# Moving every buffer that feeds TensorE to a multiple of 128 bytes in SBUF, in a fused convolution, GLU and squared-ReLU kernel

## The chip, the cores and the metric

One NeuronCore of a Trainium2 chip runs the whole program. The metric is device time in microseconds (us); lower is better. Three timed runs of the kernel before gave 2457.78, 2458.15 and 2459.22 us, so the median is 2458.15 us. The execution that the profiler recorded took 2455.46 us in all, of which the trace spans 2453.6 us.

## The reference

The input is `x` of shape (4, 4096, 192), four sequences of 4096 tokens. Three layers follow one another, all in fp32:

```python
w = softmax(weight, axis=-1)                 # (8 heads, 7 taps); 24 channels share a head
x1[s] = sum_k w[head, k] * x[s - 6 + k]      # causal convolution over the sequence, zeros before it
y   = (sigmoid(x1 @ w_gate) * (x1 @ w_val)) @ w_out          # 192 -> 1536 -> 192
out = (relu(y @ w_in2) ** 2) @ w_out2                        # 192 -> 2048 -> 192
```

Nearly all arithmetic is in the five matrix products over 16384 tokens.

## The kernel before

**Precision.** TensorE is fed with a rounded 4-byte type (`F32R`). A factor is split into a high part (the rounded value) and a low part (what rounding left), and a product is the sum of three: high by high, low of the moving operand by high weight, high by low weight. The matmuls accumulate the three in PSUM.

**Tiles.** Tokens are taken in 32 tiles of `NT = 512`. The channels lie on the partitions and the 512 tokens along them, so that one moving operand is 512 elements of 4 bytes, 2048 bytes in each partition. Every matmul of the three layers uses 64 partitions. They come in pairs: one for partitions 0 to 63, the next for 64 to 127, each with its own weights and its own PSUM bank, and the two run side by side in the two halves of the array.

**Units and phases.** A phase is one tile in one layer. A tile of the first layer (kind 1) has 12 units of 128 hidden channels, a tile of the second (kind 2) has 8 units of 256. `rows(u)` (L417) multiplies the tile's moving operand `x` with the unit's weights: 18 matmuls, that is 9 pairs. `activate(u)` (L438) turns the PSUM banks into hidden values `s` on ScalarE and VectorE, and splits them into `gh` (L455, ScalarE) and `gl` (L456, VectorE). `cols(u)` (L461) multiplies `gh` and `gl` with the output weights: 5 pairs for a unit of kind 1, 10 pairs for one of kind 2. When a phase has ended, `fold` (L485) adds the accumulators up. The program first runs three phases of kind 1, then one phase of each kind in turn, and last three phases of kind 2. The order on every engine is the order in which the program is written (`manual_schedule`): `rows` of a unit goes ahead of `cols` of a unit one or two earlier, and small works (`side`) are hung on the units.

**The moving buffers.** `operands` (L82) has two slots for the split tile `x`, each `[P, 6, 512]`. They are handed out in turn (`Slots`, L66). From the fourth phase on, the tiles of kind 1 always get the one and those of kind 2 the other, until only phases of kind 2 are left and the slots alternate. `gh` and `gl` have five buffers each. The weights lie in `w1`, `wr2` and `wo2`.

**The convolution.** `convolve` (L304) transposes the tile into `xT`, which has 6 history columns ahead of 512 new ones. `turn` copies the history in, `keep` saves the last 6 columns into a small buffer `ha`, both on GpSimd. There is one `ha` for channels 0 to 127 of the even tiles, one for those of the odd tiles, and one for the other channels. The taps follow on VectorE (L328), or, for the very first tiles, as matmuls with diagonal weights (L337, plain fp32).

**Addresses.** A pool places its buffers one behind the other in the order in which they are first asked for, each rounded up to 32 bytes. In the program before, this gives the following starts in each partition (the last column is the start modulo 128):

```
w1             16512    0        cp: small ones end at 121376  (32)
wr2            71808    0        xT of A       133664   32     2072 bytes, takes 2080
wo2            96384    0        ha (three)    24 bytes, take 32 each
x, slot 0     139936   32        xT of B       137824   96     2072 bytes, takes 2080
x, slot 1     152256   64        s  (3)   172736 ...  64
gh (5)        178880   64        gl (5)   189120 ...  64
```

Slot 0 is the one that serves the phases of kind 2 in the long middle part; slot 1 serves those of kind 1.

Of the kernel before, what the change touches and what calls it, by code (L numbers as in the profile page):

```python
# [8 lines left out]
F32 = mybir.dt.float32  # L9
# [7 lines left out]
P = 128  # L17
HB = 64
NT = 512
BLK = 32  # L20
HALVES = (slice(0, HB), slice(HB, P))


@with_exitstack
def kernel(
# [25 lines left out]
    H, K = weight.shape  # L51
    GRP = D // H
    PAD = K - 1
    F1, F2 = w_gate.shape[1], w_in2.shape[1]
    NU1, NU2 = F1 // P, F2 // (2 * P)
    TOK = B * S
# [3 lines left out]
    cp = ctx.enter_context(tc.tile_pool(name="cp", bufs=1))  # L60
    xp = ctx.enter_context(tc.tile_pool(name="xp", bufs=1))
# [113 lines left out]
    def chunk_loads(raw, srcs):  # L175
# [5 lines left out]
            )  # L181
            for half, src in zip(HALVES, srcs)
        ]
# [75 lines left out]


    xin, halo, x1, x2 = {}, {}, {}, {}

    def tokens(t):
        p, i = divmod(t, 2)
        q, j = divmod(p, TPB)
        return (2 * q + i) * S + j * NT
# [30 lines left out]
    def diagonal(i, k):  # L297
        return diag[2 * i + k // 4][:, k % 4, :]
# [5 lines left out]
    def convolve(nm, seqs, raw, j, on_array):  # L304

        i = "AB".index(nm)
        st = {}

        def turn():
            xt = st["x"] = xp.tile([P, PAD + NT], F32, tag="xT" + nm, name="xT" + nm)  # L310
            if j == 0:
                nc.vector.memset(xt[:, 0:PAD], 0.0)
            else:
                nc.gpsimd.tensor_copy(xt[:, 0:PAD], halo[nm, seqs])
            nc.vector.transpose(xt[:, PAD : PAD + NT], raw())

        def keep():
            if j < TPB - 1:
                h = halo[nm, seqs] = xp.tile([P, PAD], F32, tag=f"ha{nm}{seqs}", name="ha" + nm)
                nc.gpsimd.tensor_copy(h, st["x"][:, NT : NT + PAD])  # L320

        def first():
            st["cv"] = xp.tile([P, NT], F32, tag="cv" + nm, name="cv" + nm)
            nc.scalar.activation(st["cv"], st["x"][:, 0:NT], AF.Copy, scale=cw[:, i, 0:1])
            keep()

        def tap(k):
            nc.vector.scalar_tensor_tensor(  # L328
                out=st["cv"], in0=st["x"][:, k : k + NT], scalar=cw[:, i, k : k + 1],
                in1=st["cv"], op0=ALU.mult, op1=ALU.add,  # L330
            )

        def products():
            st["bank"] = banks.take("cv")
            st["cv"] = st["bank"][1]
            for k in range(K):
                nc.tensor.matmul(  # L337
                    st["cv"], diagonal(i, k), st["x"][:, k : k + NT],
                    start=(k == 0), stop=(k == K - 1),
                )  # L340
            keep()

        if on_array:
            return st, [turn, products]
        return st, [turn, first] + [lambda k=k: tap(k) for k in range(1, K)]

    def done(st):
# [7 lines left out]
    def part_ops(t, into, nm, src_a, src_b, done):  # L355

        own, other = HALVES[t % 2], HALVES[1 - t % 2]

# [15 lines left out]
        def spread():  # L374
            xs = into[t][1].bitcast(F32)
            nc.sync.dma_start(out=xs[HALVES[0], 4:6, :], in_=xs[HALVES[1], 0:2, :])
            nc.sync.dma_start(out=xs[HALVES[1], 4:6, :], in_=xs[HALVES[0], 0:2, :])
            nc.sync.dma_start(out=xs[other, 2:4, :], in_=xs[own, 2:4, :])
# [38 lines left out]
    def rows(u):  # L417
# [7 lines left out]
        for i, (c, o, p) in enumerate(steps):  # L425
            for h, half in enumerate(HALVES):
                nc.tensor.matmul(  # L427
# [33 lines left out]
    def cols(u):  # L461
# [4 lines left out]
        if u.f == 0:  # L466
            acc[key] = [[banks.take(f"acc{nm}") for nm in "AB"] for _ in HALVES]
        sums = acc[key]
# [238 lines left out]
```

## Time and profile before

| | |
|---|---|
| median of three timed runs | 2458.15 us |
| the profiled execution | 2455.46 us, span 2453.6 us |
| PE busy | 2395.8 us, 98% of the span, 20512 matmuls |
| PEld busy (weight loads) | 1936.4 us, 79% |
| DVE, ACT, POOL busy | 69%, 53%, 1% |
| granted TensorE clock, mean | 0.992 of full speed |

Busy time of PE is modelled and neighbouring matmuls overlap: one matmul of 64 by 512 is shown with about 390 ns, though a new pair starts every 0.23 us. The pace of TensorE is therefore read from starts, or from the chain of waits, where each piece is as long as it kept the chain. PE names matmuls and PEld the weight loads before them; `x` is the split tile, `pg`, `pv` and `ph` are PSUM banks of `rows`, `accA` and `accB` those of `cols`.

### The profile page before, as it was taken

Reading aid. Unit: us, or ns where it says so; the run is one execution under the profiler, and the core shown is the slowest. Engines: PE = TensorE matmul, PEld = TensorE weight load, DVE = VectorE, ACT = ScalarE, POOL = GpSimd, SP = SyncE. Lnnn points to the kernel's source line nnn. Section 1 sums busy time; section 2 is a strip of 40 time slices with the busy share of each in tenths; the row PEclk is TensorE's granted clock in tenths of the full one; section 3 lists DMA queues with packets and bytes.
Section 4 is the critical chain, followed back from the end, with each engine's and each line's share of the span. In section 5 each row is a group of like instructions: output and inputs, shape, how many; then the busy total and the mean of one; then the engine's idle time right before and its main releaser. Section 6 shows DMA issues by size and latency. Waiting matters only on the chain.

```text
span 2453.6 us, 49309 instructions
## 1 busy us (share of the span) xinstructions
PE 2395.8 (98%) x20512; PEld 1936.4 (79%) x20512; DVE 1704.9 (69%) x2676; ACT 1308.5 (53%) x2260; POOL 24.8 (1%) x97
## 2 busy tenths in 40 slices
PE   6898999999999999999999999999999999999998
PEld 3576888888888888888888888888888888888886
DVE  5776767676776766767676776766767676776676
ACT  5555555554555554555554555554555554555564
POOL 1000000000000000000000000000000000000000
PEclk8999999999999999999999999999999999999999
DMA  6232111112111121211112111121211112111111
GB/s 126 65 78 57 40 23 31 33 34 42 38 21 35 29 38 38 40 23 31 33 34 42 38 20 36 29 38 38 41 22 31 34 33 42 38 21 27 25 35 27
DMA packets 226896, 92.12 MB, mean 38 GB/s; under 512 B 202857, under 2 KB 214257, under 8 KB 226673
## 3 DMA queue, kind: packets, MB, share of 16 engines
q1 hardware_dynamic: 226272, 88.39, 17.8%
q8 instruction: 160, 2.62, 0.4%
q0 software_dynamic: 256, 0.52, 0.1%
q14 instruction: 64, 0.52, 0.1%
q10 hardware_dynamic: 144, 0.07, 0.0%
HBM read 26.03 MB, written 12.58 MB: 16 GB/s over the span
## 4 chain that ended last, share of the span: by engine, by line
PE 91%; DVE 4%; ACT 2%; issue 1%; DMA 1%; SPq 0%; DVEq 0%; ACTq 0%
PE pg L427 29%; PE accA L479 24%; PE ph L427 22%; PE accB L479 16%; DVE s L445 1%; ACT gh L455 1%; PE pv L427 1%; DVE gl L456 1%; DVE cvA L328 0%; DMA raw<-in_moe_w_out_dram 0%; ACT s L444 0%; DMA x<-x 0%; PE cv L337 0%; DVE cvB L328 0%; DVE w L168 0%
## 5 line engine op out<-in xcount | busy, mean ns | idle before, releaser
L427 PE MATMUL pg<-x,w 64*128 64x512 f32 x3456 | 866.3, 393 | 26.5 <-ACT w L157 22.4
L427 PE MATMUL pv<-x,w 64*128 64x512 f32 x3456 | 863.1, 393 | 14.2 <-DMA x<-x 10.3
L455 ACT CAST gh<-s 128x512 fp32r<-128x512 f32 x896 | 555.6, 621 | 520.0 <-DVE s L445 401.6
L456 DVE TENSOR_TENSOR gl<-s,gh 128x512 fp32r<-128x512 f32 x896 | 608.0, 692 | 286.2 <-ACT gh L455 264.0
L427 PEld LDWEIGHTS pg<-x,w 64*128 64x128 f32 x3456 | 639.3, 186 | 168.4 <-ACT w L157 27.1
L427 PEld LDWEIGHTS pv<-x,w 64*128 64x128 f32 x3456 | 639.7, 186 | 31.6 <-DVE s L445 11.6
L427 PE MATMUL ph<-x,wr 64*128 64x512 f32 x4608 | 573.4, 391 | 0.0
L427 PEld LDWEIGHTS ph<-x,wr 64*128 64x128 f32 x4608 | 431.9, 184 | 103.1 <-DVE s L445 0.4
L448 DVE TENSOR_TENSOR s<-s 128x512 f32<-128x512 f32 x512 | 330.3, 686 | 150.6 <-ACT s L447 149.7
L479 PE MATMUL accA<-gh,wo 64*128 64x512 f32 x2048 | 402.8, 390 | 0.0
L447 ACT ACTIVATE s<-ph 128x512 f32<-128x512 f32 x512 | 277.5, 594 | 214.6 <-PE ph L427 213.9
L445 DVE TENSOR_TENSOR s<-pv,s 128x512 f32<-128x512 f32 x384 | 263.2, 685 | 184.5 <-ACT s L444 184.0
L444 ACT ACTIVATE s<-pg 128x512 f32<-128x512 f32 x384 | 228.1, 594 | 245.5 <-PE pv L427 238.0
L479 PE MATMUL accA<-gh,w 64*128 64x512 f32 x1536 | 312.0, 390 | 0.0
L479 PEld LDWEIGHTS accA<-gh,wo 64*128 64x128 f32 x2048 | 192.3, 184 | 44.4
L479 PE MATMUL accA<-gl,wo 64*128 64x512 f32 x1024 | 200.4, 388 | 0.0
L479 PE MATMUL accB<-gh,wo 64*128 64x512 f32 x1024 | 200.4, 388 | 0.0
L479 PE MATMUL accB<-gl,wo 64*128 64x512 f32 x1024 | 199.9, 387 | 0.0
L479 PEld LDWEIGHTS accA<-gh,w 64*128 64x128 f32 x1536 | 157.5, 185 | 31.6 <-ACT gh L455 0.2
L479 PE MATMUL accA<-gl,w 64*128 64x512 f32 x768 | 158.5, 389 | 0.2 <-DVE gl L456 0.2
L479 PE MATMUL accB<-gh,w 64*128 64x512 f32 x768 | 158.0, 388 | 0.0
L479 PE MATMUL accB<-gl,w 64*128 64x512 f32 x768 | 157.9, 388 | 0.0
(92 smaller groups left out, 1442.4 us busy)
## 6 DMA issues: line engine op xcount, KB each, us to landing
x<-x SPq DMA_DIRECT2D x192, 256.0 KB, 3.8
out_dram<-oA SPq DMA_DIRECT2D x128, 64.0 KB, 2.0
xiA<-in_x_dram SPq DMA_DIRECT2D x124, 64.0 KB, 3.6
out_dram<-oB SPq DMA_DIRECT2D x64, 64.0 KB, 2.0
xiB<-in_x_dram SPq DMA_DIRECT2D x60, 64.0 KB, 2.8
rawr<-in_moe_w_in_dram SPq DMA_DIRECT2D x16, 192.0 KB, 3.4
rawo<-in_moe_w_out_dram SPq DMA_DIRECT2D x16, 192.0 KB, 2.5
raw<-in_moe_w_gate_dram SPq DMA_DIRECT2D x12, 192.0 KB, 3.3
```

Of the source, the lines that this page charges most:

```text
L427: nc.tensor.matmul(u.banks[h][1], w[half, o + c * P : o + (c + 1) * P], xs[1][half, place[c][h] + p, :], start=(i == 0), stop=(i == len(st ...
L444: nc.scalar.activation(s, u.banks[0][1], AF.Sigmoid)
L445: nc.vector.tensor_tensor(s, u.banks[1][1], s, op=ALU.mult)
L447: nc.scalar.activation(s, u.banks[i][1], AF.Relu)
L448: nc.vector.tensor_tensor(s, s, s, op=ALU.mult)
L455: nc.scalar.copy(v.gh, s)
L456: nc.vector.tensor_tensor(v.gl, s, v.gh.bitcast(F32), op=ALU.subtract)
L479: nc.tensor.matmul(sums[h][b][1], wt[half], m[half], start=(first and k in (0, 3)), stop=(last and k in (2, 4)),)
```

## The change

The transposed tile `xT` is made 544 columns wide instead of 518 (2176 bytes), of which the columns behind 518 are never touched. The three history buffers become one buffer `halos` of `[P, 3, 6]`, and it is taken from the pool of constants `cp`. No instruction is added, removed or moved, and none works on other elements than before; only addresses differ.

```diff
+LINE = 32
...
+    XT = NT + LINE * -(-PAD // LINE)
...
     xin, halo, x1, x2 = {}, {}, {}, {}
+    halos = cp.tile([P, 3, PAD], F32, name="halos")
...
         def turn():
-            xt = st["x"] = xp.tile([P, PAD + NT], F32, tag="xT" + nm, name="xT" + nm)
+            xt = st["x"] = xp.tile([P, XT], F32, tag="xT" + nm, name="xT" + nm)
...
         def keep():
             if j < TPB - 1:
-                h = halo[nm, seqs] = xp.tile([P, PAD], F32, tag=f"ha{nm}{seqs}", name="ha" + nm)
+                h = halo[nm, seqs] = halos[:, 2 * "AB".index(nm) + seqs, :]
                 nc.gpsimd.tensor_copy(h, st["x"][:, NT : NT + PAD])
```

## Rows read from the trace of the kernel before

**Rows 1.** The page: busy time of each engine, share of the span.
```profile
span 2453.6 us, 49309 instructions
PE 2395.8 (98%) x20512; PEld 1936.4 (79%) x20512; DVE 1704.9 (69%) x2676; ACT 1308.5 (53%) x2260; POOL 24.8 (1%) x97
```

**Rows 2.** The page: the chain that ended last, by engine.
```profile
PE 91%; DVE 4%; ACT 2%; issue 1%; DMA 1%; SPq 0%; DVEq 0%; ACTq 0%
```

**Rows 3.** Busy time by stage: microseconds and number of instructions, granted clock, DMA share.
```profile
30.00:90.00 60.00, 38.66 (x247) 25.61 (x245) 35.40 (x70) 32.77 (x46) 0.69 (x4) 0.86 0.45 104
90.00:250.00 160.00, 143.35 (x1138) 111.58 (x1140) 116.51 (x225) 84.29 (x153) 1.07 (x6) 0.97 0.24 61
250.00:2330.00 2080.00, 2080.00 (x18088) 1696.37 (x18088) 1451.84 (x2215) 1107.43 (x1912) 16.71 (x71) 1.00 0.17 33
2330.00:2454.00 124.00, 114.64 (x999) 93.26 (x996) 82.40 (x128) 68.02 (x118) 0.00 (x0) 0.97 0.16 32
```

**Rows 4.** The chain in order of time: start, microseconds, engine, buffer, line, instructions.
```profile
319.63 4.20 PE ph L427 x36
2306.83 4.20 PE ph L427 x36
2341.96 4.12 PE ph L427 x36
2376.78 4.19 PE ph L427 x36
2411.90 4.12 PE ph L427 x36
```

**Rows 5.** Timeline of PE in a phase of kind 1: start, microseconds, line.
```profile
1022.26 0.39 PE L427 MATMUL pg<-x,w 64*128 64x512 f32 x1
1024.32 0.39 PE L479 MATMUL accA<-gh,w 64*128 64x512 f32 x2
1025.46 0.39 PE L427 MATMUL pg<-x,w 64*128 64x512 f32 x1
```

**Rows 6.** Stages of 1.3 and 3 us: the granted clock stands after POOL's column.
```profile
93.30:94.60 1.30, 1.30 (x8) 1.00 (x6) 1.30 (x3) 0.00 (x0) 0.00 (x0) 0.50 0.00 0
28.30:31.30 3.00, 3.00 (x8) 1.32 (x7) 1.89 (x4) 0.58 (x2) 0.00 (x0) 1.00 0.00 0
```

**Rows 7.** Timeline in the first of these two stages.
```profile
93.33 0.62 PE L427 MATMUL pg<-x,w 64*128 64x512 f32 x1
93.75 0.62 PE L427 MATMUL pg<-x,w 64*128 64x512 f32 x1
94.18 0.62 PE L427 MATMUL pg<-x,w 64*128 64x512 f32 x1
94.61 0.54 PE L427 MATMUL pg<-x,w 64*128 64x512 f32 x1
```

**Rows 8.** Timeline in the second: plain fp32 matmuls, by their weight loads.
```profile
28.80 0.19 PEld L337 LDWEIGHTS cv<-xTA,diag 128*128 128x128 f32 x1 [0.24 <-issue]
...
30.94 0.19 PEld L337 LDWEIGHTS cv<-xTA,diag 128*128 128x128 f32 x1 [0.24 <-issue]
```

**Rows 9.** Timeline of DVE before the fourth `rows` of that phase.
```profile
1017.36 0.69 DVE L492 TENSOR_TENSOR ca<-accA,ca 128x512 f32<-128x512 f32 x1 [1.99 <-ACT ca L490]
...
1020.57 0.69 DVE L445 TENSOR_TENSOR s<-pv,s 128x512 f32<-128x512 f32 x1 [0.55 <-ACT s L444]
```

**Rows 10.** Groups of instructions by form: count, busy microseconds, mean nanoseconds of one.
```profile
L366 DVE TENSOR_TENSOR x<-y,x 128x512 fp32r<-128x512 f32 x32 | 21.9, 684 | 0.0
L366 DVE TENSOR_TENSOR x<-cvA,x 128x512 fp32r<-128x512 f32 x31 | 21.2, 684 | 0.7 <-ACT x L361 0.7
```

**Rows 11.** Instructions of the taps' line: minimum, median, maximum in nanoseconds.
```profile
L328 DVE SCALAR_TENSOR_TENSOR cvA<-xTA,cw,cvA x186: 737/745/752, 8.6 to 2245.4; 128x512 f32<-128x512 f32 x186
```

**Rows 12.** Instructions of `turn` and `keep` on POOL, in the same columns.
```profile
L314 POOL COPY xTA<-haA x28: 188/189/522, 32.1 to 2167.5; 128x6 f32<-128x6 f32 x28
L320 POOL COPY haA<-xTA x28: 188/189/370, 10.6 to 2038.4; 128x6 f32<-128x6 f32 x28
```

**Rows 13.** Waits, longest in total: microseconds, times, the longest one.
```profile
PEld pg L427 <- ACT w L157: 27.1, 10, 9.8
PE pg L427 <- ACT w L157: 22.4, 10, 9.4
PEld pv L427 <- DVE s L445: 11.6, 21, 1.8
PE pv L427 <- DMA x<-x: 10.3, 3, 5.6
```

## Prediction, made before the changed kernel was run

> **What bounds the kernel now.** I read the page first: PE is busy 98% of the span, the next engine, DVE, 69% [rows 1], and the chain that ended last is 91% PE [rows 2]. Busy time of PE is modelled, so I next asked whether PE ever stops. The stages say where: from 250 to 2330 us it is busy without a gap, at the full granted clock of 2.4 GHz, with 18088 matmuls or 9044 pairs in 2080 us, that is 230.0 ns for a pair [rows 3]. Before 250 us it does stop, mostly for converted weights: two rows of the waits put 49.5 us on ScalarE's L157 [rows 13]. So 85% of the time is the number of pairs times the pace of a pair, and the change can only be worth what it does to that pace.
>
> The columns alone would take 512 / 2.4 GHz = 213.3 ns. A pair takes 16.7 ns more, and the rows show four things about this excess.
>
> First, it depends on the buffer. The phases of kind 2 in the middle read `x` at start 32 modulo 128 and take 4.20 us for 36 matmuls, 18 pairs: 233.3 ns [rows 4]. In the last three phases the slots alternate: the first and third of them read slot 1, at start 64, and the same line with weights from the same buffer takes 4.12 us, 228.9 ns; the one between is back on slot 0 and at 4.19 [rows 4]. No instruction differs, only the address. The `gh` and `gl` at 64 and the `x` of kind 1 at 64 give the same 228.9: nine pairs of `rows` from 1022.26 to 1024.32 us, and 228.6 for the 14 pairs of a whole unit, to 1025.46 [rows 5].
>
> Second, at half clock it is not there. In a stretch with the clock at 0.50, which is 1.2 GHz, a new pair starts every 0.427 us [rows 6, 7]; 512 / 1.2 is 426.7. A fixed number of cycles per pair would have shown.
>
> Third, matmuls that take each column at half rate don't have it: the plain fp32 convolution at full clock steps by (30.94 - 28.80) / 5 = 0.428 us [rows 6, 8], against 1024 / 2.4 = 426.7 ns, whatever tap it is on (its starts are 32, 36, ... 56 modulo 128). So 1 to 2 ns is all that a matmul costs beyond its columns.
>
> The excess thus belongs to the supply of the moving operand, which falls behind only where TensorE takes four bytes a cycle and partition at 2.4 GHz, and which cares where the operand starts.
>
> **The change part by part.** *The addresses.* Small buffers of `cp` end at 121376, 32 modulo 128. `halos` is 72 bytes, rounded to 96, so the next pool begins at 121472, which is 949 times 128. In it the three `ha` (32 bytes each) are gone, both `xT` take 2176 = 17 x 128 bytes, and every other buffer is a multiple of 2048 bytes. Hence both slots of `x`, all `gh`, `gl` and `s` come to start at 0 modulo 128; the weights stay there. The total grows by 192 bytes.
>
> *The pace at 0.* No row shows it, so it is bounded. From below: the columns and the 1 to 2 ns, about 215.4. From above: 228.9, if 64 is already as good as it gets (and more, if 0 is worse; below). What decides for me is one arithmetic fit. An operand of 2048 bytes that starts on a multiple of 128 touches 16 blocks of 128 bytes; at any other start it touches 17. If the supply works in such blocks, each worth 32 columns, a misplaced operand takes 17 x 13.33 = 226.7 ns, and with the 2 ns from above 228.7: the rows have 228.9. (At 32 there are 4.4 ns more that this does not explain.) At 0 it is 16 blocks: 213.3 + 2.2 = 215.5. I take 215.6.
>
> [...]
>
> *The sum.* Middle: 9044 x (230.0 - 215.6) = 130.2 us. Last stage: 999 matmuls, some 499 pairs in 114.64 us of PE, 229.7 each: 499 x 14.1 = 7.0 us; the 9 us behind the last matmul stay. From 90 to 250 us: 569 pairs, but PE stands waiting 160 - 143.35 = 16.7 us there and runs partly behind the conversion, so a faster pair often only waits longer; between 0 and 569 x 13.3 = 7.6 us I take a third, 2.5. From 30 to 90 us the clock is below full for much of the time and the conversion later still: nothing of at most 124 x 13.3 = 1.6 us. Together 139.7 us. The profiled execution goes from 2455.5 to 2315.8; the median shown is 2.7 us above that execution, so it goes to 2318.5.
>
> *Is the work behind PE fast enough?* The tightest place in the middle is the fourth `rows` of a phase of kind 1: its bank is free when L445 of two units earlier ends, at 1020.57 + 0.69 = 1021.26, and it starts at 1022.26 [rows 5, 9]: 1.00 us of margin. DVE is late there because of the `fold` of the phase before, whose first addition it begins at 1017.36 [rows 9]. Between that `cols` and this `rows` stand 23 pairs, which become 23 x 13.3 = 0.31 us shorter; 0.7 us are left. In the next unit 37 pairs take 0.49 us from a like margin. DVE rises from 1451.8 / 2080 = 70% to 74% [rows 3]. If I misjudge it and each of the 29 phases of that kind stalls by 0.5 us, 14.5 us are lost; that is in the range.
>
> *What the other edits cost.* DVE and ACT also meet new addresses. The split of `y` writes slot 0 and that of `cvA` slot 1, both at 684 ns [rows 10], and six taps with six starts lie within 737 and 752 ns [rows 11]: nothing, and if each of some 5000 instructions moved by 5 ns, PE would cover it as now. The copies of `turn` and `keep` all run on POOL, 188 ns each [rows 12]; with one `halos` one may have to wait for another, at most its 0.19 us, on an engine busy 1% of the time [rows 1] and tiles ahead of need. The DMAs `x<-x` held PE only three times for 10.3 us, all in the start [rows 13]; between some 10 us either way their start address gives no reason for a change: nothing.
>
> **The rivals.**
> *64 bytes are enough.* Then only slot 0 gains. For it: 64 is a finer boundary and 32 the only start in the rows that misses it. Against it: 13 ns of excess at 64 would have no cause that goes away at half clock. Thirty of the 32 phases of kind 2 run at 32, 72 pairs each: 2160 x 4.4 = 9.5 us, so 2449.
> *The excess falls in equal steps.* From 32 to 64 it falls 4.4 ns; two more such steps, to the next multiple of 128, give 220.1. Then (230.0 - 220.1) x 9044 + (229.7 - 220.1) x 499 + 2 = 96 us are saved: 2362. Two points can't exclude it.
> *Moving operand and weights collide.* All weights start at 0 modulo 128, and weight loads are busy 1696.4 of the 2080 us beside the matmuls [rows 3]. The nearer the moving operand's start to theirs, the slower: 228.9 at 64, 233.3 at 32, so 237.7 at 0. Then every pair is slower: 9044 x 7.7 + 499 x 8.0 + some 3 in the start = 77 us, so 2535, slower than before. It decides from a pace above 230.0. For it: the two points lie in that order. Against it: the fit of 17 blocks would be an accident, and the loads fill only 82% of the middle, so there is time for them between.
> *The address is nothing.* [...] The trace disagrees: 233.3 against 228.9 for the same line [rows 4]. As a mechanism of this kernel: what separates the phases in rows 4 would be the place of the slots in memory, which moves by only a few dozen bytes. Then the time stays at 2458.
>
> **How the numbers follow.** My forecast, 16 blocks, has 0.66; equal steps 0.08; 64 is enough 0.16; collision 0.06; nothing 0.04. The likeliest case's own range goes from 2308 (all of the start's 9.2 us gained, and a pace of 215.4) to 2336 (pace 216 and the 14.5 us of stalls). To leave no more than 2 in 10 out, the range has to reach over the equal steps to the case of 64 bytes: 2308 to 2450. A measurement tells from no change what is over 0.2%, 5 us. Faster by more than that is the forecast, the steps and the 9.5 us case: 0.90; the same 0.04; slower 0.06.
>
> **What would show it.** In the new trace, 36 matmuls `ph` take 3.88 us in the chain in every phase of kind 2, the first as the last; a unit of kind 1 repeats after 14 x 215.6 = 3.02 us instead of 3.20, and the middle part has 320 pairs in 69.0 us. If all pairs stand at 228.9, the blocks are of 64 bytes or less; at 220, the excess is gradual; above 230, weights are in the way. If pairs are at 215.6 but the sum is short, there will be gaps on PE that end on DVE L445 in the third to fifth unit of a phase. I am wrong altogether if the pace at 0 is not below that at 64.

## The result and the profile after

The changed kernel takes 2422.55 us (median of four runs, 2421.75 to 2424.54), the kernel before 2458.12 in the same session. The ratio is 0.9858, with a 95% interval of 0.9843 to 0.9873: 31 to 39 us faster, where 140 had been forecast. The profiled execution took 2422.73 us, 32.7 less than that of before.

The page shows the same program with less time on PE and little else changed: PE loses 32.5 us against [rows 1], no other engine moves by more than 2.5 us.

```profile
span 2420.8 us, 49309 instructions
PE 2363.3 (98%) x20512; PEld 1936.6 (80%) x20512; DVE 1702.4 (70%) x2676; ACT 1308.4 (54%) x2260; POOL 25.8 (1%) x97
```

The stages, in the columns of [rows 3], say that the middle still has no gap on PE and the full granted clock, 1.00. In the same 2080 us there are now 18356 matmuls instead of 18088: 226.6 ns for a pair instead of 230.0.

```profile
90.00:250.00 160.00, 143.76 (x1146) 111.74 (x1148) 117.16 (x225) 84.69 (x154) 1.06 (x6) 0.97 0.23 59
250.00:2330.00 2080.00, 2080.00 (x18356) 1721.83 (x18356) 1470.85 (x2248) 1126.30 (x1946) 17.73 (x71) 1.00 0.16 33
```

The chain answers to [rows 4] (L430 is the matmul's line now, L427 before). The first `ph` piece takes 4.11 us; every one after it, to the last, takes 4.08 us for 18 pairs, 226.7 ns.

```profile
245.20 4.11 PE ph L430 x36
317.77 4.08 PE ph L430 x36
...
2310.62 4.08 PE ph L430 x36
2345.07 4.08 PE ph L430 x36
2379.52 4.08 PE ph L430 x36
```

From the first of these pieces to the last the chain needed 2379.52 - 245.20 = 2134.3 us, before 2411.90 - 246.03 = 2165.9 (the last piece is in [rows 4], the first is below): 31.5 of the 32.7 us are there, and nearly all of the rest is in the start.

```profile
246.03 4.20 PE ph L427 x36
```

With every operand on the same footing the pace is also regular: in the middle nearly every step from pair to pair lies between 226 and 228 ns. Before, the steps at start 64 mostly went around in threes of 226, 229 and 232 ns.

The timeline of a phase of kind 1 answers to [rows 5] and [rows 9]: a unit of 14 pairs repeats after 3.17 us. L448 (L445 before) ends at 1009.12 and the `rows` that needs its bank starts at 1010.07, so 0.95 us of the old 1.00 us of margin are left.

```profile
1010.07 0.39 PE L430 MATMUL pg<-x,w 64*128 64x512 f32 x1
1013.24 0.39 PE L430 MATMUL pg<-x,w 64*128 64x512 f32 x1
```

```profile
1008.43 0.69 DVE L448 TENSOR_TENSOR s<-pv,s 128x512 f32<-128x512 f32 x1 [0.55 <-ACT s L447]
```

### The profile page after: what moved, and what is told of

Same layout as the page of the kernel before. It is cut to its first block, busy times and chain, and to the rows that moved or that the text cites. A ratio compares the mean times of both kernels' runs of the same rounds, so it can differ in the third digit from the quotient of the medians.

```text
span 2420.8 us, 49309 instructions
## 1 busy us (share of the span) xinstructions
PE 2363.3 (98%) x20512; PEld 1936.6 (80%) x20512; DVE 1702.4 (70%) x2676; ACT 1308.4 (54%) x2260; POOL 25.8 (1%) x97
## 4 chain that ended last, share of the span: by engine, by line
PE 91%; DVE 4%; ACT 2%; DMA 1%; issue 1%; SPq 0%; DVEq 0%; ACTq 0%
PE pg L430 29%; PE accA L482 24%; PE ph L430 21%; PE accB L482 16%; DVE s L448 1%; PE pv L430 1%; ACT gh L458 1%; DVE gl L459 1%; DMA x<-x 0%; DMA raw<-in_moe_w_out_dram 0%; DVE cvA L331 0%; ACT s L447 0%; PE cv L340 0%; DVE cvB L331 0%; DVE w L170 0%
## 5 line engine op out<-in xcount | busy, mean ns | idle before, releaser
L430 PE MATMUL pg<-x,w 64*128 64x512 f32 x3456 | 859.3, 391 | 26.9 <-ACT w L159 22.8
L430 PE MATMUL pv<-x,w 64*128 64x512 f32 x3456 | 855.9, 391 | 14.3 <-DMA x<-x 10.1
L430 PEld LDWEIGHTS pg<-x,w 64*128 64x128 f32 x3456 | 638.5, 186 | 160.8 <-ACT w L159 27.4
L430 PEld LDWEIGHTS pv<-x,w 64*128 64x128 f32 x3456 | 639.6, 186 | 33.1 <-DVE s L448 12.2
L430 PE MATMUL ph<-x,wr 64*128 64x512 f32 x4608 | 559.3, 386 | 0.1
L430 PEld LDWEIGHTS ph<-x,wr 64*128 64x128 f32 x4608 | 432.5, 184 | 90.4 <-DVE s L448 0.5
L448 DVE TENSOR_TENSOR s<-pv,s 128x512 f32<-128x512 f32 x384 | 263.2, 685 | 174.2 <-ACT s L447 173.3
```

The source lines that it names most:

```text
L430: nc.tensor.matmul(u.banks[h][1], w[half, o + c * P : o + (c + 1) * P], xs[1][half, place[c][h] + p, :], start=(i == 0), stop=(i == len(st ...
L448: nc.vector.tensor_tensor(s, u.banks[1][1], s, op=ALU.mult)
```

## The experiments

What had to be explained is a pace that is better than at 64, but 11 ns above 215.6. Two questions: what are the 13.3 ns that remain above the columns (213.3 ns for 512, at the 0.417 ns a column that the grid below shows), and what does the start of an operand have to do with it.

**All buffers moved together, and bare stretches.** Two kernels are the changed one with a larger history buffer, which shifts every moving buffer (`keep` uses the first `PAD` columns of each part):

```diff
-    halos = cp.tile([P, 3, PAD], F32, name="halos")
+    halos = cp.tile([P, 3, 10], F32, name="halos")      # all32;  all64: 13
```

The third is no longer the program: it copies some input into a moving and a weight buffer and runs stretches of matmul pairs, one line each, with one thing changed in each stretch. In the names of stretches, m is the number of bytes by which the moving start was moved, w that of the weights (shortened; `mo` and `wo` stand for the offsets in elements):

```python
for i, h in [(i, h) for i in range(64) for h in range(2)]:
    nc.tensor.matmul((p0, p1)[h][0:128, 0:512], wt[HALVES[h], wo + i % 6 * P : ...],
                     mv[HALVES[h], mo + i % 3 * NT : ...], start=(i == 0), stop=(i == 63))
```

> The changed kernel with the history buffer 32 bytes larger, so that all moving buffers start at 32 modulo 128. If the start of the operand alone sets the pace, every pair takes 233.3 ns as the phases of kind 2 did before: (233.3 - 226.7) x 9540 pairs = 63 us above the changed kernel, about 2486, and slower than before by 28. If the order in memory or the slots matter instead, the time stays near 2423.

Measured: 2490.12 us (2488.41 to 2490.83), ratio to the kernel before 1.013 [1.0115, 1.0145]. The chain has 4.20 us for 18 pairs in every phase:

```profile
324.11 4.20 PE ph L430 x36
2446.50 4.20 PE ph L430 x36
```

> The changed kernel with the history buffer 64 bytes larger: all moving buffers at 64 modulo 128, as slot 1, gh and gl were before. If the start alone sets the pace: 228.9 for every pair, (228.9 - 226.7) x 9540 = 21 us above the changed kernel, about 2444. This is the case that the prediction called 64 bytes are enough. If it is the mixture of starts that costs, it equals the changed kernel, 2423.

Measured: 2445.99 us (2444.56 to 2448.85), ratio 0.9955 [0.9939, 0.9972], 4.12 us in every phase. Both times are within 5 us of what the start alone foretells. In this kernel the change of the time is the number of pairs times the change of a pace that addresses set; the mixture of starts is not at fault.

```profile
318.95 4.12 PE ph L430 x36
2400.92 4.12 PE ph L430 x36
```

> Not the program's computation: 25 stretches of 64 matmul pairs each, at one line each, with buffers that hold a part of the input, nothing else running beside them. One thing changes from stretch to stretch. Known: 226.7 ns a pair with all buffers at 0 modulo 128; before the change 228.9 at 64 and 233.3 at 32. Theory A, weights: the 226.7 are the two weight loads of a pair, one after the other, 113.3 ns each, and a moving start off 128 adds to that. Then weights of 64 columns instead of 128 (c64) bring the pair down to about 215.6, a single matmul on all 128 partitions (k128) takes 215.6 or less above its columns, and 256 moving columns (n256) leave the pair at 226.7. Theory B, moving operand: the 13.3 ns above the columns are part of reading 2048 bytes, whatever the weights are: c64 and k128 stay at 226.7, and n256 falls to half, about 113 to 120. Start of the moving operand, both theories: m32 233.3, m64 228.9; if what counts is the rest to the next multiple of 128, m96 lies below m64 (some 227.5) and m4 and m16 above m32; if it is the distance from the weights' start, m96 equals m32, and with weights moved along (m64w64, m32w32) the pace is 226.7 again, and with weights alone moved (w32, w64) it is slower.

Measured (steps from the ninth pair of a stretch on): m0, with a moving start on a multiple of 128, did **not** give 226.7 but 232.4; m32 234.3, m64 233.3, m96 233.4, m112 226.7, m4 240.0. With the weights moved instead, w64 gave 229.0 and w32 233.4; with both moved together, m32w32 and m64w64 gave 233.4, near m0. The premise of this run was wrong, and that was the find: a moving start on a multiple of 128 is not enough. In this kernel the two buffers start 128 bytes apart modulo 256; in the changed kernel `w1`, `wr2`, `wo2` and all moving buffers start at 128 modulo 256, so 0 apart.

Theory A fell. A single matmul on 128 partitions (k128: 232.2) and one on 64 partitions alone (one: 232.2) step as a pair does, so two loads one after the other don't set the pace. Theory B is not shown either: half the columns (n256) took 118.7 ns, inside the 113 to 120 put down for it, but 12 above their columns, so the excess hardly shrinks with the operand. Weights of 64 columns (c64) took 229.3, neither the 215.6 of theory A nor the pace of m0. In bf16 a pair takes 215.8 ns, at start 0 (bf) as at 32 (bfm32). The timeline shows the starts of these stretches (64 pairs each): (33.70 - 18.83) / 64 = 232.3 for m0 and (345.45 - 331.62) / 64 = 216.1 for bf16.

```profile
18.83 0.39 PE L56 MATMUL p_m<-mv,wt 64*128 64x512 f32 x1
33.70 0.40 PE L62 MATMUL p_m<-mv,wt 64*128 64x512 f32 x1
...
331.62 0.39 PE L184 MATMUL q_bf<-mb,wb 64*128 64x512 bf16 x1
345.45 0.38 PE L190 MATMUL q_bfm<-mb,wb 64*128 64x512 bf16 x1
```

**The distance, in the kernel and on a grid.** One more shift, `halos` of `[P, 3, 18]`, keeps all moving buffers on multiples of 128 but takes them 128 bytes from the weights.

> The changed kernel with the history buffer 128 bytes larger. All moving buffers still start on multiples of 128, but the weights stay where they were, so that moving operand and weights now differ by 128 modulo 256 instead of 0. Theory C, the distance between the two starts modulo 256 sets the pace (in the bare stretches a distance of 128 gave 232.4 ns and 240 gave 226.7): (232.4 - 226.7) x 9540 = 54 us above the changed kernel, about 2477, slower than before. Theory D, a multiple of 128 for the moving operand is what counts: 2423 as the changed kernel.

Measured: 2477.45 us (2476.19 to 2479.09), ratio 1.0083 [1.0067, 1.01]: theory C to the microsecond, and a kernel that obeys the rule in the change's words and is slower than before. The phases of kind 2 take 4.17 to 4.19 us.

```profile
319.13 4.19 PE ph L430 x36
2432.86 4.19 PE ph L430 x36
```

> Not the program's computation: 70 stretches of 40 matmul pairs, buffers with a part of the input. Moving and weight buffers both start at 0 modulo 512; the moving start is moved by m bytes, the weight start by w, or both by s. Theory C (distance m - w modulo 256): m0 226.7, m32 233.3, m64 228.9, m128 232.4, m240 226.7; m256, m288 and m320 as m0, m32 and m64; w192 as m64, w224 as m32, w128 as m128; all s as m0. Theory D (the moving start alone): all w as m0, and s32 as m32. If weight loads take time from the reading of the moving operand, 32 columns of weights (c32) bring the pair nearer to 215.8 than 96 columns do, at every start, and shorter operands (n384, n256, n128) keep the same excess of 13 ns over their columns for each pair; if it is a loss that grows with the bytes of the moving operand, n256 has half of it. Reading the same weights or the same operand each time (samew, samem) changes nothing in either.

Measured, in ns a pair from the ninth on, by m - w modulo 256 (in brackets the same distance by moving the weights, or by 256 more):

```
  0  226.7 (m256 226.7; s64, s96, s128 226.7; s32 226.8)   160  234.2 (w96 234.2)
 32  233.4 (w224 233.4, m288 233.3)                        192  233.3 (w64 233.3)
 64  228.9 (w192 228.9, m320 228.9, s32m96 228.9)          224  233.3 (w32 233.3)
 96  233.3 (w160 233.3)                                    240  226.7 (w16: 233.3)
128  232.6 (w128 232.2, m384 232.3)                         16  231.7 (w240: 226.7)
```

For 512 columns and starts on multiples of 32 the distance fixes the pace to about 1 ns, whichever buffer is moved (the largest departure is s64m192, 233.3 at distance 128). On odd multiples of 16 it does not (240 and 16 above; with both moved by 16 a pair took 230.0), and starts between cost up to 240 (m20). No start goes below 226.7. The timeline has the first matmul of each stretch, 40 pairs apart: 9.06 us for m0 (18.39 to 27.45), 9.34 for m32, 9.17 for m64 and for w192.

```profile
18.39 0.39 PE L55 MATMUL q<-mv,wt 64*128 64x512 f32 x1
27.45 0.39 PE L61 MATMUL q<-mv,wt 64*128 64x512 f32 x1
36.72 0.40 PE L67 MATMUL q<-mv,wt 64*128 64x512 f32 x1
46.06 0.39 PE L73 MATMUL q<-mv,wt 64*128 64x512 f32 x1
55.38 0.39 PE L79 MATMUL q<-mv,wt 64*128 64x512 f32 x1
64.55 0.39 PE L85 MATMUL q<-mv,wt 64*128 64x512 f32 x1
...
324.98 0.39 PE L253 MATMUL q<-mv,wt 64*128 64x512 f32 x1
334.15 0.39 PE L259 MATMUL q<-mv,wt 64*128 64x512 f32 x1
```

The columns show what remains at distance 0: 384 moving columns take 173.3 ns and 256 take 120.0. From 256 to 512 each column adds (226.7 - 120.0) / 256 = 0.417 ns, 2.4 columns a ns, and at this rate all three lengths take 13.33 ns above their columns. So at distance 0 it is the time of 32 columns for these three lengths. (128 columns take 111.6, where this would give 66.7; no run shows what holds them.) But distance 0 is the best only for 512 columns: 384 take the same 173.3 at 32, and 256 take less away from 0, 117.8 at 32 here, 118.7 at 128 and 117.3 at 160 in the bare stretches before. The timeline has 40 pairs of 256 columns at distance 0 in 546.26 - 541.48 = 4.78 us and at 32 in 550.98 - 546.26 = 4.72.

```profile
541.48 0.28 PE L397 MATMUL q<-mv,wt 64*128 64x256 f32 x1
546.26 0.28 PE L403 MATMUL q<-mv,wt 64*128 64x256 f32 x1
550.98 0.21 PE L409 MATMUL q<-mv,wt 64*128 64x128 f32 x1
```

Fewer columns of weights did not help at distance 0: 231.7 with 32 and 230.0 with 64 or 96, against the 226.7 of 128. Elsewhere they can: at distance 160, in `m1_pace`, 64 columns of weights took 226.7 (c64m32) where 128 took 234.3 (m32), 14.53 against 14.98 us for 64 pairs. So the weight load has a part in the pace beyond its start address. The same weights or the same operand each time, at distance 0: 226.7.

```profile
63.97 0.40 PE L74 MATMUL q_m<-mv,wt 64*128 64x512 f32 x1
78.95 0.40 PE L80 MATMUL q_m<-mv,wt 64*128 64x512 f32 x1
...
227.54 0.39 PE L146 MATMUL q_c64m<-mv,wt 64*64 64x512 f32 x1
242.07 0.39 PE L152 MATMUL q_c64m<-mv,wt 64*64 64x512 f32 x1
```

**Each part of the change alone, and the weights moved.** The third kernel here is the kernel *before* with two filler buffers around the weights; no moving buffer changes its start modulo 128. (One element of each filler is written in the start.)

```diff
+    ahead = cp.tile([P, 16], F32, name="ahead")          # w64
     w1 = cp.tile([P, NU1, 2 * N1], F32R, name="w1")
...
     wo2 = cp.tile([P, 2 * NU2, 2 * NO], F32R, name="wo2")
+    behind = cp.tile([P, 48], F32, name="behind")
```

> The change without the wider xT: only the three history buffers become one in the pool of constants. All moving buffers then start 64 bytes behind the weights, modulo 256. Theory C (distance of the two starts modulo 256): 228.9 ns a pair as in all64, so 2446. If each part of the change gives its share of the 36 us, about 2440.

Measured: 2444.65 us (2444.51 to 2445.94), ratio 0.9952 [0.9937, 0.9967], 4.12 us in every phase, as theory C has it.

```profile
320.19 4.12 PE ph L430 x36
2402.16 4.12 PE ph L430 x36
```

> The change without halos: only xT becomes 544 columns wide, the history buffers stay as before. gh, gl and the x of kind 1 then start at distance 0 from the weights, the x of kind 2 at 224. Theory C: 233.3 for the 2160 pairs at 224 and 226.7 for all others, so 2160 x 6.67 = 14.4 us above the changed kernel, 2437. Theory D (multiple of 128 of the moving buffers alone) gives the same here.

Measured: 2440.94 us (2438.53 to 2442.32), ratio 0.9935 [0.992, 0.995].

```profile
244.58 4.20 PE ph L427 x36
2395.18 4.08 PE ph L427 x36
```

> The kernel before with 64 bytes ahead of the weights and 192 bytes behind them: the weights start 64 bytes later, and every moving buffer 256 bytes later, which leaves its start modulo 128 as it was (x of kind 2 at 32, all others at 64). Theory C: distance 0 for all but the x of kind 2, which is at 224, as in xt_only: 2437, 21 us faster than before. Theory D: the moving starts are those of before, so 2458.

Measured: 2442.74 us (2440.17 to 2444.04), ratio 0.9942 [0.9926, 0.9959]. This is the run that decides: with the moving starts of the kernel before, the pace is that of `xt_only`, 4.20 us in the phases at distance 224, 4.08 in the last phase, whose `x` is in slot 1 at distance 0:

```profile
247.96 4.20 PE ph L429 x36
321.02 4.20 PE ph L429 x36
2398.56 4.08 PE ph L429 x36
```

Theory D is gone. `w64` and `xt_only` lie 4 to 6 us above their 2437; in both the pairs of `cols` of kind 2 average 227.3 where all at one distance have 226.7, mostly in the steps behind a `rows` at 224, which is 2 us of it. From the first `ph` piece to the last both need 2150.6 us, 16.3 more than the changed kernel: the 14.4 that were put down and these 2. What is left lies outside this stretch. The two parts of the change don't add up (12 and 15.5 us alone, 36 together, with the same kernel before): each only puts starts somewhere.

**Other patterns of reading.** Again stretches of 40 pairs, at distance 0 where nothing else is said.

> Not the program's computation: stretches of 40 pairs with other patterns of reading. The moving operand is one element 512 times (one_el), a run of 64 or 8 elements over and over (rep64, rep8), or every second element (step2); or the weights are one element 128 times (w_one_el, w_one_el_m32). Supply theory: reading the moving operand has no time to spare at 2.4 GHz, and each weight load takes at least 13.3 ns of it; where the moving operand needs fewer different lines (one_el, rep8) the pair falls to about 215.8, with every second element it becomes slower than 226.7, and with one-element weights the 13.3 ns go and the start at 32 costs nothing. Switch theory: 13.3 ns is what a change of 4-byte weights takes, whatever is read: all stay at 226.7, step2 apart.

Measured, from the ninth pair on: one_el 215.8, rep8 216.5, rep64 226.7, step2 453.4, w_one_el 231.1 and w_one_el_m32 231.1. The starts of the stretches, in the timeline: one_el takes 45.41 - 36.77 = 8.64 us for its 40 pairs, 216.0 ns, step2 81.28 - 63.16 = 18.12 us, 453 ns.

```profile
36.77 0.38 PE L67 MATMUL q<-mv,wt 64*128 64x512 f32 x1
45.41 0.39 PE L73 MATMUL q<-mv,wt 64*128 64x512 f32 x1
54.50 0.38 PE L79 MATMUL q<-mv,wt 64*128 64x512 f32 x1
63.16 0.62 PE L85 MATMUL q<-mv,wt 64*128 64x512 f32 x1
81.28 0.41 PE L91 MATMUL q<-mv,wt 64*128 64x512 f32 x1
90.54 0.39 PE L97 MATMUL q<-mv,wt 64*128 64x512 f32 x1
99.80 0.39 PE L103 MATMUL q<-mv,wt 64*128 64x512 f32 x1
```

The switch theory fell: with the same weights loaded as ever, an operand of a single element steps like bf16 (215.8 ns both), so that of the 13.3 ns only 2.5 are left. The excess thus goes with reading the moving operand, and reading every second element doubles both, columns and excess (453.4 = 2 x 226.7). But the supply theory is only half right: weights of one element did not free the 13.3 ns (231.1), though with them the start at 32 costs nothing more (231.1 as well). So for 512 columns the part above 226.7 comes from moving operand and weights together, by their distance, though no run shows by what mechanism; the 4.4 ns that one-element weights themselves add to 226.7 have no explanation here. Why 32 columns remain at distance 0 was not found; that each operand is read 32 columns further than it is long would fit 512, 384 and 256 columns and step2 at distance 0, but it is only argued, and it does not fit the 128 columns or the 117.3 to 118.7 of 256 columns at other distances.

## Why the prediction was wrong

*What bounds the kernel* was right: the pace of pairs, nothing else. PE has no gap in the middle, all64 and all32 came out as pairs times pace, and the waits for weights at the start stayed (PEld `pg` on ScalarE: 27.4 us, before 27.1 [rows 13]).

*The supply of the moving operand* as the cause of the excess was right in part, and the three observations it rested on (four were announced) stand [rows 4 to 8]. The prediction took full speed as 2.4 GHz, though the views give the clock only as a share of it; what the runs show is 2.4 columns a ns in the grid, and half of that, 512 columns in 426.7 ns, at a clock of 0.50 [rows 6, 7]. The experiments add that the excess goes, but for 2.5 ns, when one element is read over and over (one_el, 215.8), and in bf16 (215.8). But that the supply cares where the operand starts was half of it: the pace depends on where the operand starts relative to the weights (226.7 ns at distance 0, 233.4 at 32), and by what mechanism, no run shows.

*The addresses* came out as worked out: both slots of `x`, `gh`, `gl` and `s` at 0 modulo 128. That they also lie at 128 modulo 256, as the weights do, was luck: nothing in the prediction asked for it, and the same rule with the buffers 128 bytes further gave all128, 21 us slower than the kernel before instead of 36 faster.

*The pace at 0* is the step that failed: "At 0 it is 16 blocks: 213.3 + 2.2 = 215.5." Measured: 226.7, which is 17 blocks, with the operand on a multiple of 128. The fit of 17 blocks to the 228.9 at start 64 was an accident of 0.2 ns: the 226.7 are there at every start on a multiple of 32 whose distance to the weights is 0 (s32 to s128), 384 and 256 columns take their columns + 32 there too, and the 2.2 ns at 64 and 6.7 at 32 come from the distance to the weights. One number, with one unknown in it, was taken for a proof that misplacement costs a block; that the operand is read in blocks of 128 bytes was the author's assumption, and no run shows it. The 4.4 ns at start 32, which the text itself had left unexplained, were the sign that the start worked in another way. So the pieces of `ph` took 4.08 us instead of the 3.88 foretold and a unit of kind 1 3.17 instead of 3.02, a pace between the cases that the prediction had listed. The middle of the sum was 9044 x 14.4 = 130.2 us; with the measured pace it is 9044 x (230.0 - 226.7) = 30 us. The last stage shrinks by 499 x 3.0 = 1.5 us instead of 7.0, and in the start some 1 us was gained instead of 2.5. (The lower end of the range comes to 2310 by its own terms, not 2308; nothing hangs on it.)

*The margin behind PE* held; at the smaller gain it had less to bear. DVE and ACT at the new addresses and the copies with `halos` cost nothing, as said: DVE's busy time moved by 2.5 us of 1705, ACT's by 0.1, POOL's by 1.0.

*The rivals.* "64 bytes are enough" has the right kind of size (2449, all64 2446) but the wrong mechanism: 0 is better than 64. "Equal steps" foretold 220.1, and it was 226.7. "The address is nothing" fell: addresses alone moved this kernel between 2423 and 2490 us. "Moving operand and weights collide" named the right partner and the wrong sign: the pace does follow the distance, but at 512 columns it is best at 0 and worst at 160, and a slower kernel exists, though not at distance 0 where it was foretold (all128, 2477; all32, 2490). Its chance of 0.06 was too low for a reason that could have been seen: every weight start was the same in the trace of before, so no row there could tell a moving start from a distance.

*What the runs leave open.* bf16 (215.8) and one_el (215.8) came within 0.2 ns of the 215.6 foretold; `F32R` operands of 512 different elements never got there in any run here, and no run shows why. In w64 only the weights moved modulo 256, by 64 bytes, and the kernel was 14 us faster; whether it is bandwidth that loading the weights and reading the moving operand share, no run shows either.

None of the kernels run is faster than the changed one, and no start of the grid has a lower pace at 512 columns, so the runs point to no better placement for this kernel.

## What to carry to other kernels

Where TensorE is the bound and takes 4-byte operands at full rate, compare the step from pair to pair with its columns (0.417 ns each in the grid), and sort it by the buffers' start addresses, weights included: here 3% of the time lay between distances of 0 and 32 bytes modulo 256. With operands of 512 columns and starts on multiples of 32, place moving operands and weights at the same start modulo 256 (226.7 ns a pair here, against 228.9 to 234.2 at the other distances in steps of 32); at 256 columns the same distance was the slowest of the four measured (120.0 against 117.3 to 118.7), so measure other lengths first. Check the starts after every edit that adds a small buffer ahead of them, since a pool passes 32 bytes on to all that follow. When a fit of one number decides a forecast, look for a second quantity that it must also explain; here the next row had it.

## What was not expected of the hardware

- At distance 0, `F32R` matmuls take the time of 32 more columns than they have: 226.7, 173.3 and 120.0 ns for 512, 384 and 256 (226.7 also in the changed kernel, where the granted clock was 1.00). At other distances 256 columns took 117.3 to 118.7.
- At 512 columns the pace differs by up to 7.5 ns with the distance between moving operand and weights modulo 256, at multiples of 32; at a start off by 4 or 20 bytes a pair took 238.4 and 240.0 ns.
- With half 0 at distance 0 and half 1 at 64 (one stretch of the grid) a pair stepped by 226.7, not 228.9.
- Weights of 64 columns instead of 128 took a pair from 234.3 to 226.7 ns at distance 160, and from 226.7 to 230.0 at distance 0.
